# Eight weight tiles loaded ahead, two FFN tiles in the accumulators' PSUM banks, and a later start of batch 1's attention

## The chip, the cores and the metric

The kernel runs on one NeuronCore of a Trainium2 chip. The metric is device time in microseconds (us) of one execution; a kernel is told by the median of its runs. TensorE is called PE here, VectorE DVE, ScalarE ACT, GpSimd POOL and SyncE SP, as in the profile. Every bulk load and store is issued from SP's queue, in order.

## The reference

Inputs are q, k, v (8 batches, 8 heads, 576 positions, 64 per head), 32 packed queries p per head, and two FFN matrices w_in (512 x 2048) and w_out (2048 x 512). In short:

```
p_packed = softmax(p @ k.T / 8) @ v                      # 32 rows per head
a        = softmax(q @ p_packed.T / 8) @ p_packed        # 576 rows per head
x        = heads of a side by side                       # 4608 x 512
out      = softplus(x @ w_in) @ w_out                    # float32
```

The data are float64 in memory (the weights are read as int64 words); the result is float32.

## The kernel before

**Weights.** w_in and w_out come as 16 tiles each of 128 x 512 float64 values, 512 KB a tile, and are turned to float32 on the core by `convert` (L173): ACT reads the two halves of each word (`first`: L200 writes m, L204 writes r), DVE builds sign and exponent (L206, L211), POOL adds (L219) into `w_in_sb` or a scratch tile t; for w_out, ACT rounds t to `wo_h` (L238) and DVE takes the remainder `wo_l` (L244). Tiles are numbered n = 0 to 31 in the order i0 i1 o0 o1 i2 i3 o2 o3 i4 i5 and so on. `prefetch` loads a tile into one of the places of the list `places` (L180): two buffers "x" and two stretches of the tile `rest`, which batch 0's softplus fills only later. When `first(n)` has read a place, the place is loaded again as long as n is below its entry in `until`.

**Attention.** For each batch, attention runs in a generator (`attention_first` for batches 0 and 1): it transposes the heads of k (`psT_k` on PE, copied to `T_k` by ACT, L268), takes scores against p, a softmax over 576 positions, packs v, then the same for q (`psT_q`, `T_q`) with a softmax over 32 columns on DVE. k and v of batch 0 lie in the four buffers of the pool `ld`, q of batch 0 in a part of `w_in_sb` not yet used; batch 1's k and v take the same four buffers. `weights` splits the result into `at_h` (ACT, L525) and `at_l` (DVE, L526).

**FFN.** For each batch there are 16 units f. `make_m` (L535) folds p_packed into w_in: `psm` on PE (L543), split into `mh` by ACT (L558) and `ml` by DVE (L559); for batch 0 one call serves two units. `gemm1` (L564) makes `ph` in two halves of 288 columns, 12 matmuls (L580). `softplus` (L597) is Abs (L602), Exp (L604) and Ln (L605) on ACT, then max-and-add on DVE (L607), which is the last reader of `ph`, then the split into `gh` and `gl` (L594, L595); POOL saves 64 columns (L611). Two units later (LAG) `gemm2_tile` (L616) adds gh, gl times wo_h, wo_l into four accumulators `acc`, 12 matmuls of 512 columns (L618).

**PSUM.** There are eight banks: four for `acc` (pool `ps_acc`), two for `ph` (pool `ps_h`, tag "h"), two for everything else (pool `ps_m`, tag "m": `psm`, `psT`, scores, `psa`, `psp`, `psx`). During attention 0 the six banks of `ps_acc` and `ps_m` are lent in turn (`bank`, L87); `spare.clear()` (L712) ends that.

**Order of the work.** PE's order is the order of the program text. In the main loop (L717) each unit has four t-steps; at each one gemm2 tile is issued, `due` grows by PACE (0.56; in batch 1's units by PACE_FIRST, 0.62) and, whenever it passes 1, one step of the next batch's attention is issued; in batch 0 `cdue` grows by 1.6 and issues steps of `convert`. The other engines' order is chosen by the framework's scheduler from that program; each engine then works its queue strictly in order.

Of the kernel before, what the change touches and what calls it, by code (L numbers as in the profile page):

```python
# [9 lines left out]
F32 = mybir.dt.float32  # L10
# [5 lines left out]
I64 = mybir.dt.int64  # L16
# [10 lines left out]
def pack_attention_then_softplus_ffn(  # L27
# [14 lines left out]
    P = 128  # L42
# [4 lines left out]
    G = H * J // P  # L47
    HG = H // G
    NF = DFF // P
    NT = S // P  # L50
    REST = S - NT * P
    LAG = 2
    MC = 512
    Q = 32
    FIRST = 2
# [3 lines left out]
    ld = ctx.enter_context(tc.tile_pool(name="ld", bufs=2 * G))  # L59
# [3 lines left out]
    ps_acc = ctx.enter_context(tc.tile_pool(name="ps_acc", bufs=NT, space=bass.MemoryType.PSUM))  # L63
    ps_h = ctx.enter_context(tc.tile_pool(name="ps_h", bufs=2, space=bass.MemoryType.PSUM))
# [82 lines left out]
    CN = 512  # L147

    def load64(srcs, nm, place):
        if place is None:  # L150
            x = cv.tile([P, CN], I64, tag="x", name=f"x_{nm}", bufs=2)
        else:
            x = rest[:, place:place + 8, :].rearrange("x f j -> x (f j)").bitcast(I64)
        n = P // len(srcs)
        for i, src in enumerate(srcs):
            nc.sync.dma_start(
                x[i * n:(i + 1) * n].rearrange("x (a n) -> x a n", a=src.shape[1]), src
            )
        return x
# [13 lines left out]
    def convert(order):  # L173
# [3 lines left out]

        srcs = {"i": w_in_src, "o": w_out_src}

        places, until = [None, None, LAG, LAG + 8], [len(order), len(order), 6, 16]  # L180
        xs, ts, rs, at = {}, {}, {}, {}

        def prefetch(place):
# [39 lines left out]
        for n in range(2):  # L223
            prefetch(n)
        yield
        for n in range(2, 4):
            prefetch(n)
        yield
        for n in range(len(order) + 1):
# [6 lines left out]
            t = ts.pop(n - 1)[0].bitcast(F32) if n else None  # L236
# [327 lines left out]
    def gemm1(b, f, res):  # L564

        n = m_cols(b)
        halves = res["m"][f * P // n]
        at_h, at_l = res["at"]
        phs = []
        for c in range(2):  # L570
            ph = ps_h.tile([P, 512], F32, tag="h", name=f"ph_{b}_{f}_{c}")
            phs.append(ph[:, :C])
            i = 0
            for g in range(G):
                mh, ml = halves[g * n // MC]
                o = g * n % MC + f * P % n
                ms = slice(o, o + P)
                cs = slice(c * C, (c + 1) * C)
                for x, y in ((mh, at_h), (mh, at_l), (ml, at_h)):
                    nc.tensor.matmul(  # L580
                        ph[:, :C], x[:, ms], y[:, g, cs],
                        start=(i == 0), stop=(i == 3 * G - 1),
                    )
                    i += 1
        return phs
# [83 lines left out]
    order = []  # L669
# [4 lines left out]
    PACE = 0.56  # L674
    FRONT = 1000
    PACE_FIRST = 0.62
    CONV = 1.6
    CONV_EARLY = 1.6
    CONV_STEP = 14
# [15 lines left out]
    due = 0.0  # L695
# [18 lines left out]
    gs, acc = {}, None  # L714
    units = [(b, f) for b in range(B) for f in range(NF)]
    ahead, chain, due = iter(()), iter(()), 0.0
    for u in range(len(units) + LAG):  # L717
        if u < len(units):
            b, f = units[u]
            if f == 0:  # L720
                if (b + 1) % BG == 0 and b + 1 < B:
                    pack_transposed((b + 1) // BG, pt)
                ahead = attention(b + 1) if b + 1 < B else iter(())
                due = 0.0
            chain = softplus(b, f, gemm1(b, f, res[b]), gs)
            next(chain)
            if f == NF - 1:
                if (b + 2) % BG == 0 and b + 2 < B:
                    pt = load_pack((b + 2) // BG, (nc.sync,))
                for _ in ahead:  # L730
                    pass
                if b + 1 < B:
                    weights(b + 1)
        if u >= LAG:
            b2, f2 = units[u - LAG]
            gh, gl = gs.pop((b2, f2))
            if f2 == 0:
                acc = [ps_acc.tile([P, DM], F32, tag="acc", name=f"acc_{b2}_{t}") for t in range(NT)]
        last = u >= LAG and f2 == NF - 1 and b2 % 2 == 1
        if last:  # L740
            both = rests(b2)
            next(both)
        for t in range(NT):
            if u >= LAG:
                gemm2_tile(
                    acc[t], gh, gl, f2, slice(t * P, (t + 1) * P), f2 == 0, f2 == NF - 1
                )
                if f2 == NF - 1:
                    store(acc[t], [(0, b2, t * P, P)], f"{b2}_{t}", t)
            if u < len(units):  # L750
                due += PACE if b != FIRST - 1 else PACE_FIRST
                while due >= 1:
                    next(ahead, None)
                    due -= 1
                if b == 0:
                    cdue += CONV
                    while cdue >= 1:
                        next(conv, None)
                        cdue -= 1
            next(chain, None)  # L760
        if last:
            next(both)
        if u + 2 < len(units):


            nb, c = units[u + 2][0], units[u + 2][1] * P
            if c % m_cols(nb) == 0:
                make_m(nb, c // m_cols(nb), res[nb])
# [29 lines left out]
```

## Time and profile before

| | |
|---|---|
| runs | 777.18, 774.43, 775.15 us; median 775.15 |
| profiled execution | 774.48 us, its span 772.7 us (1.8 us lie around the span) |
| busy over the span | PE 94%, DVE 68%, ACT 56%, POOL 13% |
| mean granted PE clock | 0.985 |

Times in the views are us from the span's start. A row of the timeline has start, duration, engine, line, operation, output and input; a bracket tells the idle time ahead of it on its engine and who ended that. A row of the stages has, for each engine, the busy us and the number of instructions; PEclk is the granted clock, 1.00 being full speed. A row of the waits has total us, times, and the longest.

### The profile page before, as it was taken

The page shows a single profiled execution, that of the slowest core. Times are in us where ns is not written, and L with a number is a line of the kernel's source. Part 1 is how long each engine was busy: PE and PEld are TensorE (multiplying, and loading weights), DVE is VectorE, ACT ScalarE, POOL GpSimd, SP SyncE. Part 2 cuts the span into 40 slices and gives each one's busy share as a digit, 9 for nine tenths or more (in the row PEclk, how much of TensorE's full clock was granted, in tenths as well). Part 3 has the DMA queues.
Part 4 walks back from the last instruction along what each step waited for, and adds up shares of the span by engine and source line. Part 5 has one row for each costly group of instructions (what it writes and reads, how often), then busy time and mean ns, then how long its engine had stood idle before and what let it go on. Part 6 is the DMA issues. An engine that isn't in the chain of part 4 may idle for free.

```text
span 772.7 us, 14153 instructions
## 1 busy us (share of the span) xinstructions
PE 729.3 (94%) x5360; PEld 577.0 (75%) x5360; DVE 527.4 (68%) x1092; ACT 435.3 (56%) x1057; POOL 99.0 (13%) x166
## 2 busy tenths in 40 slices
PE   6457997999999999999999999999999999999997
PEld 4346675687788778877887777878787777888886
DVE  2697869975877559575877559576877558565554
ACT  5667977666455445565555455565555355555540
POOL 1253434200000000000010000000010000000110
PEclk9969999999999999999999999999999999999999
DMA  9977644534302342052402332043401400010002
GB/s 205 247 194 179 180 133 125 120 74 78 76 17 68 63 68 57 1 116 47 87 0 69 62 63 62 1 98 51 92 1 55 75 2 1 1 55 1 1 1 68
DMA packets 149668, 55.97 MB, mean 72 GB/s; under 512 B 116320, under 2 KB 142944, under 8 KB 149600
## 3 DMA queue, kind: packets, MB, share of 16 engines
q1 hardware_dynamic: 149328, 55.00, 31.9%
q8 instruction: 42, 0.69, 0.4%
q14 instruction: 26, 0.21, 0.1%
q10 hardware_dynamic: 272, 0.07, 0.0%
HBM read 45.61 MB, written 9.44 MB: 71 GB/s over the span
## 4 chain that ended last, share of the span: by engine, by line
PE 82%; DVE 6%; ACT 6%; DMA 4%; POOL 1%; issue 1%; SPq 0%; ACTq 0%; DVEq 0%; POOLq 0%
PE acc L618 41%; PE ph L580 26%; PE acc_m L618 6%; PE psm L543 4%; PE ps L275 2%; DMA w_in_sb<-in_q 2%; PE psp L318 1%; PE psa L308 1%; DMA k<-in_k 1%; ACT m L200 1%; DVE at_l L526 1%; DVE t L211 1%; POOL t L219 1%; ACT e L604 1%; DVE t L206 1%
## 5 line engine op out<-in xcount | busy, mean ns | idle before, releaser
L602 ACT ACTIVATE e<-ph 128x288 f32<-128x288 f32 x256 | 103.1, 404 | 189.3 <-PE ph L580 142.4
L618 PE MATMUL acc<-wo_h,gh 128*128 128x512 f32 x512 | 207.6, 405 | 0.0
L607 DVE SCALAR_TENSOR_TENSOR e<-ph,e 128x288 f32<-128x288 f32 x256 | 113.3, 451 | 131.9 <-ACT e L605 128.2
L618 PE MATMUL acc<-wo_l,gh 128*128 128x512 f32 x512 | 200.9, 392 | 0.0
L618 PE MATMUL acc<-wo_h,gl 128*128 128x512 f32 x512 | 200.8, 392 | 0.0
L580 PE MATMUL ph<-at_h,mh 128*128 128x288 f32 x512 | 158.9, 310 | 14.8 <-ACT at_h L525 7.5
L580 PE MATMUL ph<-at_l,mh 128*128 128x288 f32 x512 | 153.3, 299 | 3.7 <-DVE at_l L526 3.7
L580 PE MATMUL ph<-at_h,ml 128*128 128x288 f32 x512 | 152.7, 298 | 0.0
L580 PEld LDWEIGHTS ph<-at_h,mh 128*128 128x128 f32 x512 | 97.6, 191 | 48.8 <-DVE e L607 10.8
L611 POOL COPY rest<-e 128x64 f32<-128x64 f32 x128 | 53.2, 416 | 575.8 <-DVE e L607 544.2
L618 PEld LDWEIGHTS acc<-wo_h,gh 128*128 128x128 f32 x512 | 96.2, 188 | 27.4 <-issue 10.2
L618 PEld LDWEIGHTS acc<-wo_h,gl 128*128 128x128 f32 x512 | 96.1, 188 | 21.0
L604 ACT ACTIVATE e<-e 128x288 f32<-128x288 f32 (+1 forms) x240 | 109.5, 456 | 3.9
L605 ACT ACTIVATE e<-e 128x288 f32<-128x288 f32 (+1 forms) x240 | 109.4, 456 | 3.2
L618 PEld LDWEIGHTS acc<-wo_l,gh 128*128 128x128 f32 x512 | 96.4, 188 | 13.0
L580 PEld LDWEIGHTS ph<-at_l,mh 128*128 128x128 f32 x512 | 97.8, 191 | 8.2 <-DVE at_l L526 5.3
L580 PEld LDWEIGHTS ph<-at_h,ml 128*128 128x128 f32 x512 | 97.8, 191 | 0.0
L595 DVE TENSOR_TENSOR gl<-e,gh 128x512 fp32r<-128x512 f32 x128 | 87.7, 685 | 5.5
L558 ACT CAST mh<-psm 128x512 fp32r<-128x512 f32 (+1 forms) x72 | 35.9, 540 | 53.5 <-PE psm L543 53.4
L594 DVE CAST gh<-e 128x512 fp32r<-128x512 f32 x128 | 55.5, 434 | 5.1
L559 DVE TENSOR_TENSOR ml<-psm,mh 128x512 fp32r<-128x512 f32 (+1 forms) x72 | 42.8, 623 | 20.2 <-ACT mh L558 19.6
L543 PE MATMUL psm<-w_in_sb,pt 64*32 64x512 f32 (+1 forms) x576 | 40.0, 560 | 9.7 <-ACT T_k L268 4.8
(79 smaller groups left out, 693.5 us busy)
## 6 DMA issues: line engine op xcount, KB each, us to landing
v<-in_v SPq DMA_DIRECT2D x16, 576.0 KB, 5.0
x_i<-in_moe_w_in SPq DMA_DIRECT2D x28, 256.0 KB, 4.5
k<-in_k SPq DMA_DIRECT2D x48, 144.0 KB, 3.1
q<-in_q SPq DMA_DIRECT2D x48, 144.0 KB, 3.2
x_o<-in_moe_w_out SPq DMA_DIRECT2D x11, 512.0 KB, 3.8
out<-o SPq DMA_DIRECT2D x18, 256.0 KB, 2.5
rest<-in_moe_w_out SPq DMA_DIRECT2D x5, 512.0 KB, 6.0
k<-in_k SPq DMA_DIRECT2D x4, 576.0 KB, 6.5
```

The lines of the kernel that those rows point to most:

```text
L543: nc.tensor.matmul(ps[hh * J:(hh + 1) * J, :n], res["pt"][g][o:o + D, hh * J:(hh + 1) * J], w_in_sb[o:o + D, hh, c * n:(c + 1) * n], start ...
L558: nc.scalar.copy(mh[:, cols], ps[:, :n])
L559: nc.vector.tensor_tensor(ml[:, cols], ps[:, :n], mh[:, cols].bitcast(F32), op=ALU.subtract)
L580: nc.tensor.matmul(ph[:, :C], x[:, ms], y[:, g, cs], start=(i == 0), stop=(i == 3 * G - 1),)
L594: nc.vector.tensor_copy(hi, x)
L595: nc.vector.tensor_tensor(lo, x, hi.bitcast(F32), op=ALU.subtract)
L602: nc.scalar.activation(es[c], hv[c], AF.Abs)
L604: nc.scalar.activation(x, x, AF.Exp, scale=-1.0)
L605: nc.scalar.activation(x, x, AF.Ln, bias=1.0)
L607: nc.vector.scalar_tensor_tensor(es[c], hv[c], 0.0, es[c], op0=ALU.max, op1=ALU.add)
L611: nc.gpsimd.tensor_copy(rest[:, rest_at(b, f), r:r + REST], e[:, NT * P:])
L618: nc.tensor.matmul(acc, x[:, cs], y[:, f, :], start=(first and i == 0), stop=(last and i == 2),)
```

## The change

Three things are changed.

1. **Places for weight tiles.** The list gets four more entries, "ld", which are the four buffers of k and v of batch 0 (a tile of the pool `ld`, tag "ld"). At the start n = 0, 1 go to "x", n = 2, 3 to `rest`, and n = 4 to 7 (i2, i3, o2, o3) each to a buffer of k or v as soon as batch 0's attention has read that for the last time. These four are used once (`until` 0). The first stretch of `rest` is not loaded again (`until` 2 instead of 6). The places "x" then hold n = 8 and 9 where they held 4 and 5.
2. **Banks.** `ph` of units 0 and 1 of batch 0 is taken from `ps_acc` instead of `ps_h`.
3. **Pace.** In batch 0's units, which issue batch 1's attention, `due` does not grow in the first 8 t-steps (AFTER), so that attention starts with unit 2 instead of unit 0; from there it grows by PACE_FIRST (0.62) per t-step instead of PACE (0.56). Batch 1's units keep 0.62 and the later ones 0.56.

What it moves on PE: batch 1's first transposes of k stand in unit 2 instead of behind unit 0, its second scores of the first half (`scores2`, g = 0) at the end of unit 10 instead of unit 9, those of the second half in unit 13 instead of 12. The six later `psm` pairs of batch 0 (pairs 2 to 7) each stand directly behind another user of the two "m" banks; before, three of the seven pairs from 1 on did so (1, 3 and 5). The rows below show PE and ACT at the places that matter; the names are the program's, with the batch's or unit's number behind them.

PE, from the end of unit 0's gemm1, before (`k` is batch 1's; `psm_1` feeds units 2 and 3):

```order
72 L580 MATMUL ph_0_1_534<-at_h_521,ml_0_0_516 128x288
73 L262 MATMUL psT_k_0_0_551<-ident,k_0_497 128x96 x3
74 L262 MATMUL psT_k_0_1_573<-ident,k_0_497 128x96 x3
75 L543 MATMUL psm_1_0_587<-w_in_sb,pt_0_351 32x256 x4
76 L543 MATMUL psm_1_1_588<-w_in_sb,pt_1_428 32x256 x4
77 L580 MATMUL ph_1_0_603<-at_h_521,mh_0_0_515 128x288
```

and PE from the same place in the changed kernel:

```order
72 L584 MATMUL ph_0_1_536<-at_h_523,ml_0_0_518 128x288
73 L546 MATMUL psm_1_0_575<-w_in_sb,pt_0_354 32x256 x4
74 L546 MATMUL psm_1_1_576<-w_in_sb,pt_1_430 32x256 x4
75 L584 MATMUL ph_1_0_591<-at_h_523,mh_0_0_517 128x288
76 L584 MATMUL ph_1_0_591<-at_l_524,mh_0_0_517 128x288
```

The two transposes have gone from between gemm1 of unit 0 and `psm_1`; units 1 and 2 now follow without any work of attention.

ACT, from the Ln of unit 0 on, before (m and r read weight tiles, `mh_1` is the split of `psm_1`):

```order
62 L605 ACTIVATE e_0_541<-e_0_541 128x576
63 L268 COPY T_k_0_0_555<-psT_k_0_0_551 128x288
64 L200 ACTIVATE m_557<-x_i_288 128x512
65 L204 ACTIVATE r_559<-x_i_288 128x512
66 L268 COPY T_k_0_1_577<-psT_k_0_1_573 128x288
67 L204 ACTIVATE r_581<-rest 128x512
68 L558 CAST mh_1_0_597<-psm_1_0_587 128x256
```

and ACT in the changed kernel:

```order
62 L609 ACTIVATE e_0_543<-e_0_543 128x576
63 L203 ACTIVATE m_551<-x_i_174 128x512
64 L207 ACTIVATE r_553<-x_i_174 128x512
65 L207 ACTIVATE r_569<-rest 128x512
66 L561 CAST mh_1_0_585<-psm_1_0_575 128x256
```

The two copies T_k have gone; the weight tiles' reads are the same and in the same order as before (the order of ACT, DVE and POOL is unchanged up to here).

ACT in unit 4 of the changed kernel, around the copies of the first scores (`ps_1_0_0` and `ps_1_0_1` hold both "m" banks; `psT_k_1_0`, `psT_k_1_1` and `psm_3` need them next):

```order
97 L287 COPY a_1_0_673<-ps_1_0_0_824 128x288
98 L207 ACTIVATE r_711<-x_o_620 128x512
99 L203 ACTIVATE m_709<-x_o_620 128x512
100 L608 ACTIVATE e_4_812<-e_4_812 128x576
101 L207 ACTIVATE r_771<-x_o_637 128x512
102 L609 ACTIVATE e_4_812<-e_4_812 128x576
103 L203 ACTIVATE m_769<-x_o_637 128x512
104 L241 CAST wo_h<-t_713 128x512
105 L287 COPY a_1_0_673<-ps_1_0_1_830 128x288
106 L271 COPY T_k_1_0_854<-psT_k_1_0_850 128x288
107 L271 COPY T_k_1_1_884<-psT_k_1_1_880 128x288
```

Seven instructions now stand between the two copies that set the banks free; on PE the pair `psm_3` stands directly behind `psT_k_1_1`.

```
-        if place is None:
+        if place == "x":
             x = cv.tile([P, CN], I64, tag="x", name=f"x_{nm}", bufs=2)
+        elif place == "ld":
+            x = ld.tile([P, CN], I64, tag="ld", name=f"x_{nm}")
...
-        places, until = [None, None, LAG, LAG + 8], [len(order), len(order), 6, 16]
+        places = ["x", "x", LAG, LAG + 8] + ["ld"] * 2 * G
+        until = [len(order), len(order), 2, 16] + [0] * 2 * G
...
-        for n in range(2, 4):
+        for n in range(2, len(places)):
...
-            ph = ps_h.tile([P, 512], F32, tag="h", name=f"ph_{b}_{f}_{c}")
+            pool, tag = (ps_acc, "acc") if b == 0 and f < LAG else (ps_h, "h")
+            ph = pool.tile([P, 512], F32, tag=tag, name=f"ph_{b}_{f}_{c}")
...
+    AFTER = 8
...
-                due += PACE if b != FIRST - 1 else PACE_FIRST
+                if b >= FIRST:
+                    due += PACE
+                elif b or NT * f + t >= AFTER:
+                    due += PACE_FIRST
```

## The prediction, made before the result was known

> **What bounds the kernel now.** I read the busy time by stages first, with a border where batch 1's first gemm1 starts (153.3 us).
>
> ```profile
> 43.80:61.00 17.20, 9.33 (x49) 7.26 (x50) 14.23 (x24) 11.60 (x24) 10.03 (x8) 0.70 0.85 210
> 61.00:75.40 14.40, 12.56 (x90) 9.58 (x89) 10.20 (x22) 11.69 (x26) 4.88 (x6) 0.90 0.63 164
> 75.40:126.00 50.60, 47.04 (x416) 35.46 (x417) 41.23 (x87) 41.20 (x87) 21.53 (x22) 1.00 0.57 152
> 126.00:153.30 27.30, 23.22 (x163) 16.98 (x161) 25.75 (x51) 19.12 (x38) 8.61 (x9) 1.00 0.56 125
> 43.80:153.30 109.50, 92.15 (x715) 69.28 (x715) 91.41 (x181) 83.61 (x173) 45.05 (x42) 0.94 0.62 156
> 153.30:772.70 619.40, 613.56 (x4396) 491.52 (x4396) 412.82 (x861) 325.06 (x828) 46.09 (x113) 1.00 0.23 47
> ```
>
> After 153.3 us PE is busy 613.56 of 619.4 us: that part is PE's own work, and the change touches none of it. Batch 0's FFN (43.8 to 153.3) is different: PE is idle 17.4 us of 109.5, at clock 0.94, while DVE is busy 91.41 and ACT 83.61, since weight conversion, softplus and batch 1's attention meet there. So the time moves only by as much as the 153.3 moves. Who holds PE in that stretch, by the waits of PE:
>
> ```profile
> PE ph L580 <- DVE e L607: 7.2, 4, 3.0
> PE psm L543 <- ACT T_k L268: 4.8, 2, 4.5
> PE psm L543 <- ACT T_q L268: 2.5, 2, 1.7
> PE psm L543 <- POOL w_in_sb L219: 1.7, 1, 1.7
> PE psm L543 <- ACT a1T L309: 0.7, 1, 0.7
> ```
>
> Two PSUM shortages are seen. `ph` has two banks, so a unit waits until the unit before has been read by L607 (7.2 us). `psm` shares the two "m" banks with attention and waits for ACT's copies T_k, T_q, a1T (8.0 us, and 1.7 for a weight tile; 9.7 in all). PE's timeline shows the places:
>
> ```profile
> 45.88 1.07 PE L262 MATMUL psT_k<-ident,k 96*128 96x96 f32 x6
> 51.49 1.07 PE L543 MATMUL psm<-w_in_sb,pt 64*32 64x256 f32 x8 [4.55 <-ACT T_k L268]
> 53.85 0.61 PE L580 MATMUL ph<-at_h,mh 128*128 128x288 f32 x1
> 60.64 0.61 PE L580 MATMUL ph<-at_h,mh 128*128 128x288 f32 x1 [3.05 <-DVE e L607]
> 63.45 0.44 PE L580 MATMUL ph<-at_h,ml 128*128 128x288 f32 x1
> 64.53 0.72 PE L275 MATMUL ps<-T_k,pT 64*32 64x288 f32 x16
> 66.66 0.41 PE L262 MATMUL psT_k<-ident,k 96*128 96x96 f32 x3
> 68.32 0.40 PE L580 MATMUL ph<-at_h,mh 128*128 128x288 f32 x1
> ```
>
> Unit 1 begins at 53.85, unit 2 at 60.64, unit 3 at 68.32.
>
> **Part 1, eight tiles in flight: 0.** It pays only where ACT waits for a weight tile. ACT's waits for loads from 28 to 160 us:
>
> ```profile
> ACT r L204 <- DMA x_o<-in_moe_w_out: 1.0, 1, 1.0
> ACT m L200 <- DMA x_i<-in_moe_w_in: 0.3, 1, 0.3
> ACT m L200 <- DMA rest<-in_moe_w_out: 0.2, 1, 0.2
> ```
>
> 1.5 us in all, and the longest is for a late load of w_out, whose place the change leaves as it was. The order rows show the same tiles read in the same order up to unit 1. So between 0 and 0.5 us can be gained; I take 0. It could also cost: the loads of i2 and i3 are now queued behind `rest` without waiting for ACT, and the critical chain of the first 22 us is the load of q:
>
> ```profile
> 6.90 14.82 DMA w_in_sb<-in_q
> ```
>
> The new loads stand behind q's on the same queue. If they took bandwidth from it, the part newly issued before 21.7 us (i3 and half of i2, about 0.8 MB) at the 210 GB/s of the first row would cost up to 3.7 us. I take 0, because i2 was on its way before q had landed in this run too; the upper end goes to the range. The Trainium skill (DMA: Bandwidth & Descriptors, "Two DMAs through the same engine are not ordered") says that descriptors of one queue start in order on each engine; by it q would lose nothing. No run here shows that yet.
>
> On SP's queue, behind the new waits for v's buffers (read last by `psp`), stand i4, i5, o4 and batch 1's k; all are needed only after 40 us, so no one waits.
>
> **Parts 2 and 3 in the front.** ACT, DVE and POOL around unit 0's softplus:
>
> ```profile
> 49.86 0.62 ACT L238 CAST wo_h<-t 128x512 fp32r<-128x512 f32 x1 [0.79 <-POOL t L219]
> 50.39 0.68 ACT L605 ACTIVATE e<-e 128x576 f32<-128x576 f32 x1
> 50.97 0.38 ACT L268 COPY T_k<-psT_k 128x288 f32<-128x288 f32 x1
> 51.25 0.68 ACT L200 ACTIVATE m<-x_i 128x512 f32<-128x512 f32 x1
> 51.83 0.68 ACT L204 ACTIVATE r<-x_i 128x512 int32<-128x512 uint32 x1
> 52.39 0.40 ACT L268 COPY T_k<-psT_k 128x288 f32<-128x288 f32 x1
> 51.10 0.82 DVE L607 SCALAR_TENSOR_TENSOR e<-ph,e 128x288 f32<-128x288 f32 x2
> 53.90 0.68 DVE L595 TENSOR_TENSOR gl<-e,gh 128x512 fp32r<-128x512 f32 x1
> 54.50 0.41 DVE L559 TENSOR_TENSOR ml<-psm,mh 128x256 fp32r<-128x256 f32 x1
> 65.80 0.82 DVE L607 SCALAR_TENSOR_TENSOR e<-ph,e 128x288 f32<-128x288 f32 x2 [2.04 <-ACT e L605]
> 44.48 1.32 POOL L219 TENSOR_TENSOR w_in_sb<-t,r 128x512 int32<-128x512 int32 x1 [3.63 <-DVE t L211]
> ```
>
> - Until 46.1 us (end of unit 0's gemm1) nothing changes: the orders are the same.
> - `psm_1` then runs at 46.1, where `psT_k` stood (45.88): its weights are there (POOL ends at 44.48 + 1.32 = 45.8). Two halves of 1.07 end at 48.2. Unit 1 has its own banks: 12 matmuls at (63.45 - 60.64) / 11 = 0.255 us give 51.3.
> - Unit 2 needs `ml_1`. ACT reaches `mh_1` two T_k copies (0.28 each from start to start) earlier, near 52.7; DVE still passes L607, conversion and gl first and makes the first `ml_1` at 54.5 and the second directly behind it, at 54.9. Unit 2's third matmul starts at 54.95; ten at 0.24 end it near 57.3. Before, it ended at 63.45 + 0.44 = 63.9.
> - Unit 3 needs unit 2's L607. Before, that ended at 66.62, 2.7 us behind unit 2's end. In the new order two instructions of conversion on ACT and one on DVE stand in between (0.58 + 0.53 + 0.6 = 1.7): 57.3 + 2.7 + 1.7 = 61.7. PE meanwhile does four gemm2 tiles and two transposes (57.3 to 60.7) and `psm_2`.
>
> Unit 3 starts at 61.8 instead of 68.3: 6.5 us earlier. But PE has by then done three transposes (0.25 each) and one set of scores (0.65) less of attention, 1.4 us, which comes later. **Front: -5.1 us.** The bounds: 0, if DVE and ACT hold the later units as late as before, and -6.5, if that 1.4 is hidden.
>
> The clock in the front, in stages of 2 us:
>
> ```profile
> 50.00:52.00 2.00, 0.51 (x8) 0.23 (x8) 1.88 (x5) 2.00 (x5) 1.48 (x1) 0.53 1.02 307
> 54.00:56.00 2.00, 2.00 (x9) 2.00 (x10) 1.93 (x4) 1.25 (x3) 1.60 (x1) 0.50 1.09 257
> ```
>
> After PE's pause (46.9 to 51.5) it works at about half clock, still so at 54 to 56. In the changed kernel a pause stays between units 1 and 2 (51.3 to 54.95), so I count units 1 and 2 at half clock, as measured. The Trainium skill (TensorE: Matmul & The Clock Gate, "What's actually happening") halves the clock after an idle window of about 3.4 us and restores it after a busy one of that length; the rows agree. By it the pause of 3.6 us could fall either way; at full clock unit 2 would end 1.2 us earlier and the sum would be -5.3 instead of -4.1.
>
> **Part 3 later on: the "m" banks.** Now six pairs of `psm` stand directly behind another user of the banks. What one such place costs:
>
> ```profile
> 108.56 0.64 PE L543 MATMUL psm<-w_in_sb,pt 64*32 64x256 f32 x8 [0.80 <-ACT T_q L268]
> 121.34 0.67 PE L543 MATMUL psm<-w_in_sb,pt 64*32 64x256 f32 x16 [1.71 <-ACT T_q L268]
> ```
>
> I take 0.2 for pair 2 (PE arrives late there), 0.8 for pairs 4, 5 and 7, 1.7 for pair 6 (both banks are held by scores that DVE must read), and for pair 3 this: between the two copies of the scores stand seven instructions of ACT (four m or r at 0.58, Exp and Ln at 0.58, wo_h at 0.53: 4.0 us), in which PE has three gemm2 tiles and a transpose, 2.3 us; 1.7 more of wait and 0.8 for the copies behind it, 2.5. Sum 6.8. The pairs 2 to 7 waited 9.7 - 4.8 = 4.9 before: **+1.9 us** (bounds: 0, and +5.4 if each of the six costs 1.7).
>
> **The end of batch 0.** From 126 to 153.3 DVE is busy 25.75 of 27.3 us and PE idle 4.1: the last weight tiles and the second softmax meet. In the new order that softmax begins behind the last weight tile's instruction on DVE, one unit later. 1.7 of the 4.1 is the wait for a weight tile, counted above; of the other 2.4 I take **-0.9** (bounds 0 and -2.4), as only one unit's overlap goes.
>
> Does the softmax then come too late for batch 1? Between the transposes of its scores and the second `at_l` DVE has 17 instructions of at most 0.68 and two tiny ones, under 12 us, and no conversion. PE has in that time two gemm2 tiles of unit 13, units 14 and 15, `psm` and `ppt`, with full units as here:
>
> ```profile
> 157.90 1.58 PE ph L580 x12
> 159.48 2.74 PE acc L618 x12
> ```
>
> 1.4 + 2 x 4.3 + 1.0 + 0.6 = 11.6. That is about even: 0, with up to +1.
>
> **Sum:** 0 - 5.1 + 1.9 - 0.9 = -4.1 us. The profiled execution took 774.48 (span 772.7); it would take 770.4. It lies 0.67 below the median, and I set the forecast from the median: 775.15 - 4.1 = 771.0 us. About 0.5%, 3.9 us, is what a measurement of this kernel can tell from no change, so faster means below 771.3: the forecast lies just beyond that line.
>
> **Rivals.**
> - *The lead is spent waiting (no change).* ACT and DVE have the same work in batch 0 as before, 83.61 and 91.41 us, and PE's lead only makes it wait for them in units 3 to 12. For: over 75.4 to 126 each of the two is busy 81%. Against: DVE was free 4.2 of the 14.4 us from 61 to 75.4, which the new order uses. It would give -1 to 0: 774.5.
> - *All of the front is kept and the end gains too.* Bank waits as before (4.9), the end -2.4: -5.1 - 2.4 = -7.5: 767.6. For: DVE's heavy part comes when conversion is over. Against: the pair `psm_3` in the order.
> - *The banks make it slower.* Each of the six pairs waits for ACT copies that stand behind conversion, as pair 1 did for 4.8 us. The point of no gain is a mean of (4.9 + 5.1) / 6 = 1.7 us per pair; at 3.1 the six make 18.6, so 18.6 - 4.9 - 5.1 = +8.6: 783.8; at 2.4, +4.4: 779.5, which I take as its time. For: 1.71 has been seen. Against: of the five places in the waits only one was over 1.7.
>
> **How the numbers follow.** Forecast 0.50 (its own range 768.8 to 773; 0.33 of it below 771.3), all kept 0.18, no change 0.22, slower 0.10. Faster 0.33 + 0.18 = 0.51; within 0.5% 0.17 + 0.22 = 0.39; slower 0.10. The range takes in the first three and the q term only in part: 766.2 to 775.8.
>
> **What would show it.** Right: `psm_1` within 0.5 us of unit 0's end, unit 1 directly behind it, unit 2 ending near 57 and unit 3 starting near 62; no wait for L607 before unit 1 or 2; a wait of some 2 us around `psT_k_1_1` and `psm_3`; batch 1's gemm1 starting near 149.2. Wrong: q landing later than 22 us (part 1 costs), unit 3 near 62 but batch 1 at 152 or later (the lead is spent), waits at `psm` of over 10 us (the banks), or batch 1's gemm1 waiting for `at_l`.

## The result, and the profile after

The changed kernel takes 779.16 us (median of 4 runs, 778.62 to 779.37), the kernel before 774.79 (4 runs): 1.0051 times as long (95% interval 1.0031 to 1.0071), 4.4 us slower, where I had forecast 4.1 us faster. Its profiled execution has a span of 776.8 us against 772.7.

By stages, as before, with the border where batch 1's first gemm1 starts (157.38 us now; a row has, for PE, PEld, DVE, ACT and POOL, busy us and instructions, then PE's granted clock, DMA share and GB/s):

```profile
44.60:157.40 112.80, 96.78 (x715) 73.49 (x715) 93.94 (x181) 83.97 (x173) 42.97 (x42) 0.89 0.58 147
157.40:776.80 619.40, 613.55 (x4396) 491.55 (x4396) 412.94 (x861) 325.15 (x828) 46.23 (x113) 1.00 0.23 47
```

Batch 1 begins 4.1 us later (157.38 - 153.28), and that is the whole difference of the spans: behind it PE is busy 613.55 us of 619.40, as before. All of it arises up to the end of batch 0's FFN. PE's idle time there has not grown (112.80 - 96.78 = 16.0 us, before 17.4), but PE is busy 4.6 us longer for the same number of instructions, at clock 0.89 instead of 0.94.

PE's timeline shows the front as forecast, and then the waits (in the bracket: idle before, and who ended it):

```profile
46.78 1.11 PE L546 MATMUL psm<-w_in_sb,pt 64*32 64x256 f32 x16
53.94 0.61 PE L584 MATMUL ph<-at_h,mh 128*128 128x288 f32 x1 [3.81 <-ACT mh L561]
63.23 0.40 PE L584 MATMUL ph<-at_h,mh 128*128 128x288 f32 x1
76.93 0.74 PE L265 MATMUL psT_k<-ident,k 96*128 96x96 f32 x3 [3.02 <-ACT a L287]
107.13 0.64 PE L546 MATMUL psm<-w_in_sb,pt 64*32 64x256 f32 x8 [0.71 <-ACT a1T L312]
109.84 0.68 PE L546 MATMUL psm<-w_in_sb,pt 64*32 64x256 f32 x8 [2.07 <-DVE pt L336]
126.31 0.91 PE L546 MATMUL psm<-w_in_sb,pt 64*32 64x256 f32 x16 [2.38 <-DVE a L346]
140.18 0.84 PE L546 MATMUL psm<-w_in_sb,pt 64*32 64x256 f32 x16 [0.87 <-ACT T_q L271]
```

`psm_1` follows unit 0 directly, unit 3 starts at 63.23 (before 68.32), unit 4 at 68.27 (75.37): 5.1 and then 7.1 us ahead. Behind it come `psT_k_1_1`, the two halves of `psm_5`, `psm_6` and `psm_7`, which wait 9.05 us in all for the "m" banks. The first of these is the pair of scores that the prediction named. ACT's timeline there:

```profile
71.42 0.40 ACT L287 COPY a<-ps 128x288 f32<-128x288 f32 x1 [0.29 <-PE ps L278]
71.72 0.67 ACT L207 ACTIVATE r<-x_o 128x512 int32<-128x512 uint32 x1
72.29 0.66 ACT L203 ACTIVATE m<-x_o 128x512 f32<-128x512 f32 x1
...
75.96 0.62 ACT L241 CAST wo_h<-t 128x512 fp32r<-128x512 f32 x1 [0.63 <-POOL t L222]
76.48 0.39 ACT L287 COPY a<-ps 128x288 f32<-128x288 f32 x1
```

Seven instructions stand between the two copies, which start 5.1 us apart; `psT_k_1_1` needs the second. The same in windows of 3.41 us (PE's busy us and instructions, the granted clock, DMA share, GB/s), round `psm_5`:

```profile
103.49:106.90 3.41, 2.78 (x14) 1.00 0.41 104
106.90:110.31 3.41, 1.10 (x16) 1.00 0.15 43
110.31:113.73 3.42, 3.42 (x17) 0.50 0.45 111
113.73:117.14 3.41, 3.41 (x61) 1.00 0.72 197
```

A window with much waiting is followed by one at half clock. That happens behind the waits at 76.9 (two windows), 109.8 and 126.3; in the profile of before it does not happen once behind 64 us.

From unit 3's start to batch 1, PE alone, before and then after:

```profile
68.32:153.28 84.96, 75.48 (x616) 1.00 0.59 149
```

```profile
63.23:157.38 94.15, 82.92 (x636) 0.93 0.54 140
```

The changed kernel enters this stage 5.1 us ahead and needs 9.2 us more for it: 1.75 more idle (11.23 against 9.48), 7.44 more busy. Of the latter some 1.4 is attention put off from the front; the rest, 6.0, is put down to half clock. The idle time grew by so little, in spite of the 9.05 us at the "m" banks, because other waits went: those for the product's last reader (L607, now L611) fell from 4.2 to 1.5 us here, and the wait of 1.7 us for a weight tile is gone.

### The profile page after: what moved, and what is told of

Same layout as the page of the kernel before. It is cut to its first block, busy times and chain, and to the rows that moved or that the text cites. A ratio compares the mean times of both kernels' runs of the same rounds, so it can differ in the third digit from the quotient of the medians.

```text
span 776.8 us, 14159 instructions
## 1 busy us (share of the span) xinstructions
PE 733.9 (94%) x5360; PEld 580.9 (75%) x5360; DVE 530.0 (68%) x1092; ACT 435.7 (56%) x1057; POOL 97.0 (12%) x166
## 4 chain that ended last, share of the span: by engine, by line
PE 82%; DVE 8%; ACT 4%; DMA 3%; issue 1%; POOL 1%; SPq 0%; ACTq 0%; DVEq 0%; POOLq 0%
PE acc L622 41%; PE ph L584 26%; PE acc_m L622 6%; PE psm L546 4%; PE ps L278 2%; DMA rest<-in_moe_w_out 2%; PE psp L321 1%; DVE at_l L529 1%; PE psa L311 1%; DVE t L214 1%; DMA x_i<-in_moe_w_in 1%; DVE e L611 1%; ACT e L608 1%; DVE t L209 1%; DVE gl L599 1%
## 5 line engine op out<-in xcount | busy, mean ns | idle before, releaser
L611 DVE SCALAR_TENSOR_TENSOR e<-ph,e 128x288 f32<-128x288 f32 x256 | 113.2, 451 | 132.9 <-ACT e L609 131.7
L599 DVE TENSOR_TENSOR gl<-e,gh 128x512 fp32r<-128x512 f32 x128 | 90.5, 707 | 5.6
L562 DVE TENSOR_TENSOR ml<-psm,mh 128x512 fp32r<-128x512 f32 (+1 forms) x72 | 42.6, 622 | 20.0 <-ACT mh L561 19.3
```

What stands on the lines that cost most here:

```text
L562: nc.vector.tensor_tensor(ml[:, cols], ps[:, :n], mh[:, cols].bitcast(F32), op=ALU.subtract)
L599: nc.vector.tensor_tensor(lo, x, hi.bitcast(F32), op=ALU.subtract)
L611: nc.vector.scalar_tensor_tensor(es[c], hv[c], 0.0, es[c], op0=ALU.max, op1=ALU.add)
```

## The experiments

The theory after the traces, **A**: the places directly ahead of `psm` make PE wait for the two "m" banks, the clock halves behind each wait, and that takes the front's gain back and more. The rivals: **B**, part 1 (the places of the weight tiles) costs time all through batch 0; **C**, ACT and DVE limit batch 0, so that a lead can only be spent. Each run is timed against the kernel before in the same session, and the ratio is to that.

### The three parts alone

e1_places has part 1 alone, e2_banks part 2, e3_pace part 3, e4_banks_pace parts 2 and 3. Their diffs against the kernel before are pieces of the change:

```diff
e1:
-        places, until = [None, None, LAG, LAG + 8], [len(order), len(order), 6, 16]
+        places = ["x", "x", LAG, LAG + 8] + ["ld"] * 2 * G
+        until = [len(order), len(order), 2, 16] + [0] * 2 * G
...
e2:
+            pool, tag = (ps_acc, "acc") if b == 0 and f < LAG else (ps_h, "h")
...
e3:
+    AFTER = 8
...
+                elif b or NT * f + t >= AFTER:
+                    due += PACE_FIRST
e4: the lines of e2 and e3
```

> The kernel before with the first part of the change alone: eight weight tiles in flight, the attention and the banks as before. Theory A (the m banks): the change loses behind its front, where psT_k_1_1, psm_3, psm_5 and psm_6 wait for the two m banks and the granted clock falls to half after each wait; this part adds only the 0.8 us by which gemm1 of unit 0 starts later (39.48 against 38.71): 775.6, between 774.8 and 776.6. Theory B (the places): the two weight tiles that land 0.7 to 0.9 us later push conversion back all through batch 0, and this part makes up most of the 4.4 us by which the changed kernel is slower: 777.5 or more. Theory C (the lead is only spent, since ACT and DVE limit batch 0): 774.8 to 775.6, as A.

> The kernel before with the second part alone: the gemm1 of units 0 and 1 in the accumulators' banks, the attention's places as before. psm_1 still waits 4.8 us behind psT_k_0_0 and psT_k_0_1, so that unit 1 starts no earlier; only unit 2 no longer waits for unit 0's product at L607, which stands behind psm_1's wait anyway. Theory A: -0.5 to -2 us, 773 to 774.3, since the order at the later m banks is that of before. Theory B: 774.8, no change. Theory C: 774.3 to 774.8.

> The kernel before with the third part alone: batch 1's attention begins two units later and goes at 0.62, places and banks as before. Theory A: psm_1 runs directly behind unit 0, but units 1 and 2 wait in the h banks for the products of the unit before, so that some 2 to 4 us of the front's 5.1 are won; the later m-bank waits and their half clock are those of the changed kernel (9 us lost from unit 4 on, as it was 7.1 ahead there and ends 4.1 behind less the 0.8 of its start): 778 to 781, slower. Theory B: below 776, since the places are not there. Theory C: 774 to 775.5.

> The changed kernel without its first part: six weight tiles' places as before, units 0 and 1 in the accumulators' banks, the attention later. Theory A: 0.8 us below the changed kernel, 778.0 to 778.8, with waits of 2 us or more at psT_k_1_1 or psm_3, at psm_5 and at psm_6, each with a stretch at about half clock. Theory B: 774 to 776, the loss gone with the places. Theory C: 774.8, no change.

| run | median us | ratio (95%) | unit 0 | unit 3 | batch 1 |
|---|---|---|---|---|---|
| before | 775.52 | 1 | 38.71 | 68.32 | 153.28 |
| e1_places | 778.44 | 1.0040 (1.0026 to 1.0054) | 38.21 | 69.06 | 156.20 |
| e2_banks | 782.94 | 1.0093 (1.0080 to 1.0107) | 39.12 | 64.59 | 160.97 |
| e3_pace | 782.49 | 1.0089 (1.0073 to 1.0105) | 38.63 | 65.27 | 160.44 |
| e4_banks_pace | 777.93 | 1.0035 (1.0021 to 1.0050) | 38.30 | 62.44 | 155.94 |

(Starts of gemm1 in the profiled executions.) B falls as the main cause: most of the loss is there without part 1 (e4). But e1 came out where B had put it, and above A's range: part 1 alone costs 2.9 us. In its profile they are lost late: unit 10 starts at 114.07 (before 114.61), unit 12 at 129.99 (128.82), and two windows at half clock lie there, from 123.05 and from 136.70. And what I took for part 1's cost, unit 0's late start in the changed kernel's profile (39.48), is chance: in the changed kernel, e1 and the runs e5 to e8 below, all with part 1, unit 0 starts at 38.15 to 39.48, mean 38.56; in the kernel before, e2 to e4, e9 and e10, without it, at 38.26 to 39.12, mean 38.60. Whether part 1 costs something later in the changed kernel stays open: e4 and the changed kernel differ by 1.2 us, but their intervals overlap.

The parts do not add up: 2.9 + 7.4 + 7.0 us, but 4.4 together. A met e4, missed e1 and e3 by less than 2 us, and e2 by 9 us: in e2 the attention stands where it stood before, unit 3 is 3.7 us ahead, and batch 1 is 7.7 us behind. Its first loss is not at an "m" bank ahead of `psm`:

```profile
77.88 0.72 PE L275 MATMUL ps<-T_k,pT 64*32 64x288 f32 x5 [3.29 <-ACT T_k L268]
```

So every one of these kernels with an earlier unit 3 lost that lead, and not all at the same place.

### Is it the half clock?

e8_fill adds matmuls to the changed kernel that nobody reads, in free columns of the h banks, so that PE is busy while it waits. Two stand ahead of `psT_k_1_1`, three behind `psx` and three behind the second scores. The instructions of ACT, DVE and POOL stay in the changed kernel's order.

```diff
+    def fill(b, n):
+        at_h, _ = res[b]["at"]
+        for i in range(n):
+            nc.tensor.matmul(
+                full[i % 2][:, C:], at_h[:, 0, :P].bitcast(F32),
+                at_h[:, 0, :512 - C].bitcast(F32), start=True, stop=True,
+            )
...
+                if b == 0 and t == NT - 1 and f == 4:
+                    fill(0, 2)
...
+                if b == 0 and t == NT - 1 and f in (8, 10):
+                    fill(0, 3)
```

> The changed kernel with eight more matmuls in batch 0, whose results nobody reads, in free columns of the h banks: two ahead of psT_k_1_1 in unit 4, three between psx and psm_5 in unit 8, three ahead of psm_6 in unit 10. They stand where TensorE waits (3.0, 2.8 and 2.4 us) and should take some 0.6 us each. The order on the other engines is that of the changed kernel. Theory A1 (the clock): in all six traces so far the granted clock is 0.5 for whole stretches of 3.41 us on a fixed grid, each behind a stretch of 3.41 us in which TensorE was busy for less than about 0.55 of the time. With the waits filled, the stretches at 76 (two), 110 and 127 us should stay at 1.00: 775 to 777, 2 to 4 us less than the changed kernel's 779.2. Theory A2 (only the waits cost, the clock does not matter since ACT and DVE are the limit behind them): 778.5 to 780. The matmuls of the waits run longer than the wait: 780 or more.

Measured: 778.97 us (1.0049, 1.0036 to 1.0061), no gain. The fill did what it should at `psm_5` (windows of e8_fill, as above):

```profile
108.39:111.81 3.42, 2.72 (x24) 1.00 0.28 87
111.81:115.22 3.41, 3.41 (x23) 1.00 0.40 83
```

The window with the wait is now busy for 2.72 us, and the next keeps its clock; unit 9 takes 5.8 us to unit 10 instead of 7.2. At `psT_k_1_1` it did so only in part: the fill itself stood 1.43 us until DVE had read the h bank that it writes, the window of the wait was busy for 1.57 us, and one half-clock window follows instead of two. At `psm_6` PE is let go at 126.92 (126.31 in the changed kernel), without a half-clock window behind it; and a new one turns up from 87.9, so that two are left of four. In the whole stage:

```profile
63.41:157.72 94.31, 84.15 (x652) 0.96 0.53 136
```

Less 3.82 us of fill (1.02 + 1.40 + 1.40), PE is busy 80.3 us, 2.6 less than in the changed kernel; it waits, the fill counted in, 14.0 us instead of 11.2, 2.8 more. A1 is not borne out, and A2 met the time: the half clock is real, but the 2.6 us of it that went came back as waits. That fits PE being let go at times that other engines set; with two half-clock windows left and a fill that waits for DVE itself, the run does not prove it.

### Is it the places ahead of psm?

e6_gap ("the run without adjacent steps" in what was expected of others) is the changed kernel with one condition more, e5_after4 moves the attention's start, e7_first puts the copies that free the banks ahead of conversion (five places in batch 1's attention, one shown):

```diff
e6   -                while due >= 1:
     +                while due >= 1 and not (b == 0 and t == NT - 1 and f % 2 == 0):
e5   -    AFTER = 8
     +    AFTER = 4
e7   +        with tc.high_priority(offset=FRONT) if b == 1 else ExitStack():
             nc.scalar.copy(dst, ps[:, :C])
```

> The changed kernel, but in batch 0 no step of the attention stands directly ahead of a psm: a step that falls due there runs one gemm2 tile later. The order on ACT and DVE changes with it. Theory A (the m banks): the waits at psT_k_1_1, psm_5, psm_6 and psm_7, 9.0 us in the changed kernel, fall to under 3, with one half-clock stretch at most behind unit 4: 771 to 775. Theory C (ACT and DVE limit batch 0, the lead is only spent): TensorE waits as long in other places (L611, mh, at_l): 777 to 780.

> The changed kernel with AFTER = 4: batch 1's attention begins one unit earlier (one unit later than in the kernel before), and no step of it but two transposes of k at units 2 to 4 stands directly ahead of a psm. Theory A: as in the run without adjacent steps, 771 to 776. Theory C: 777 to 780. If the attention's lateness itself is the cost: about half of the change's loss, 776 to 777.

> The changed kernel with the copies that free the m banks in batch 1's attention (ACT's copies of T, of the scores and of a1T, DVE's transposes of the second scores and its copy pt) put ahead of conversion by priority. Theory A: TensorE's waits at the m banks fall from 9.0 to some 4 us with one or two half-clock stretches less, but conversion is later: 775 to 777.5. Theory C: the same work is done in another order, 778 to 780.

Measured: e6_gap 774.26 us (0.9994, 0.9985 to 1.0004), e5_after4 775.75 (1.0014, 1.0005 to 1.0023), e7_first 778.21 (1.0043, 1.0030 to 1.0055), the kernel before 774.95. With no step directly ahead of a `psm` (e6) the change loses nothing: 4.9 us less (779.16 to 774.26), with the reservation that the edit shifts rows of ACT and DVE too. Priority for the copies does not do it, as C had it; conversion then comes late, and `psm_7` waits 3.23 us for its weights from POOL.

The stage from unit 3 to batch 1 in e6_gap:

```profile
62.40:152.81 90.41, 79.77 (x643) 0.96 0.58 145
```

It has 6.8 us at half clock, as many as e8_fill, but waits 10.6 us where that waits 14.0. Against the changed kernel's stage (94.15 us, busy 82.92) it is 3.7 us shorter: PE waits only 0.6 less and is busy 3.2 less, with two half-clock windows instead of four. Yet e6_gap gains nothing on the kernel before, though unit 3 starts 5.9 us ahead. Its largest waits behind 60 us:

```profile
PE psT_k L265 <- ACT a L287: 4.1, 1, 4.1
PE psT_q L265 <- DVE a L346: 1.6, 1, 1.6
PE ps L278 <- DVE ml L562: 1.5, 2, 1.3
```

All three wait for an "m" bank that another step or a `psm` still holds. `psm` is let through at once now, and the attention waits in its stead: `psT_k_1_1` for 4.1 us, with two half-clock windows. So A's time came, but not its signs (waits under 3 us there, one such window at most). Unit 5 is 2.5 us ahead, batch 1 0.5.

e5_after4 is a warning too. In its order a gemm2 tile stands between every step and the next `psm`, as in e6_gap, and still `psm` waits 7.5 us in all for the "m" banks; the first two of these waits:

```profile
75.95 0.64 PE L546 MATMUL psm<-w_in_sb,pt 64*32 64x256 f32 x8 [1.46 <-ACT T_k L271]
78.36 1.08 PE L546 MATMUL psm<-w_in_sb,pt 64*32 64x256 f32 x8 [1.77 <-ACT T_k L271]
```

With almost as much wait at `psm` as the changed kernel has at the banks, e5_after4 is 3.4 us faster than that. So the places are part of the loss at most; that they alone are its cause is not shown. For the lead C holds so far.

### Where does the lead go?

e9_gap6 is e6_gap without part 1; e10_gap_scores puts ACT's copies of batch 1's first scores first, which takes away the 4.1:

```diff
e9   the condition of e6 in e4_banks_pace
e10  +        with tc.high_priority(offset=FRONT) if b == 1 else ExitStack():
                 nc.scalar.copy(a1[:, c * C:(c + 1) * C], ps)
```

> The run without adjacent steps, with six weight tiles in flight as before (no part 1); the order on ACT and DVE is nearly that of that run (774.26). If part 1 costs the same here as in the changed kernel (779.16 with it, 777.93 without): 773.0, faster than the kernel before by some 0.25%. If the places cost nothing when the banks don't bind: 774.3. If the late tiles hid something, and conversion is starved without them: 775 or more.

> As the run without adjacent steps and with six tiles, and ACT's copies of batch 1's first scores go ahead of conversion. In the run without adjacent steps psT_k_1_1 still waits 4.12 us for the second copy, which stands behind four m and r and one wo_h that waits for POOL, and two half-clock stretches follow. If that wait is what spends the front's lead of 6 us: 2 to 4 us less, 769.5 to 771. If the lead is spent by ACT and DVE whatever waits first (theory C): the wait turns up again at later units, 772.5 to 774.5.

Measured: 774.84 us (0.9987, 0.9972 to 1.0002) and 774.93 (0.9987, 0.9973 to 1.0000), the kernel before 775.62. With part 1 (e6_gap, 0.9994) and without it (e9_gap6) the ratios cannot be told apart. In e10 unit 5 starts at 77.14, 5.8 us ahead of before (82.9); by unit 8 the lead is 1.6, and batch 1 starts at 155.27 in its profile, 2.0 behind. The wait taken away came back in pieces, as C said.

Which engine? e11_gap_light and e12_before_light spare DVE:

```diff
-                    wo_l[:, i, :], t, wo_h[:, i, :].bitcast(F32), op=ALU.subtract
+                    wo_l[:, i, :16], t[:, :16], wo_h[:, i, :16].bitcast(F32), op=ALU.subtract
+    nc.gpsimd.memset(wo_l.bitcast(F32).rearrange("x f e -> x (f e)"), 0.0)
```

> The run without adjacent steps, but wo_l is computed for 16 of its 512 columns only and is zero elsewhere (the low halves of the second weights are left out): 16 instructions of DVE of 0.6 us become some 0.1, about 8 us less of DVE in batch 0. Theory C, with DVE as the limit: the front's lead is kept in part, 2 to 5 us below 774.3: 769 to 772. If ACT's queue is what spends the lead: 773.5 to 775.

> The control: the kernel before with wo_l for 16 of its 512 columns only, zero elsewhere. Theory C: DVE limits the kernel before in batch 0 too, which shows as 1 to 3 us less: 772 to 774. If DVE's work is hidden there: 774.5 to 775.5. A larger gain here than in the run without adjacent steps would say that the front's lead is not spent on DVE.

Measured: 776.41 us (1.0007, 0.9994 to 1.0020) and 778.12 (1.0019, 1.0002 to 1.0037). Both are flawed by my own edit: the zeroing takes POOL 6.93 us and stands ahead of the identity matrix, so that unit 0 starts 1.6 and 2.6 us later. From unit 0 to batch 1 they take 115.7 and 116.2 us, against 114.5 (e6_gap) and 114.6 (before), though DVE is busy 7.8 and 6.7 us less in them. Sparing this work of DVE brought nothing; with the flaw, and one profile of each, that is a hint and no proof that DVE is not the limit.

e13_gap_nopool leaves out POOL's add, e14_gap_nor also ACT's `r`, both in e9_gap6; e15_before_nor and e16_after_nor are the kernel before and the changed kernel with both left out.

```diff
e13 to e16, in second(n):
+            if n >= 8:
...
+                nc.vector.scalar_tensor_tensor(
+                    o if a > 1 else o.rearrange("x (a n) -> x a n", a=a), x, 3, y,
+                    op0=ALU.logical_shift_left, op1=ALU.bitwise_or,
+                )
+                return
...
e14 to e16, in first(n):
+            if n < 8:
...
+                nc.scalar.activation(r, lo, AF.Copy, scale=2.0**-29)
```

> The run without adjacent steps and with six tiles (774.84, stage from unit 0's gemm1 to batch 1's 113.6 us in its profile), but POOL's add of the lowest three bits is left out for weight tiles 8 to 47, whose t comes from DVE's second instruction; ACT still makes r. If ACT's waits for POOL at wo_h (some 6 us behind 58 us) spend the lead: the stage is 3 to 6 us shorter, 769 to 772. If ACT's own work does: 774 to 775.5.

> As the run before, and ACT's r is left out too for tiles 8 to 47 (the weights are cut off instead of rounded in their last bits): 40 instructions of 0.58 us less on ACT, 23 us. If ACT's work spends the lead: 4 to 8 us below the run that only leaves out POOL's add, 766 to 770. If neither does, since each unit waits for a chain through all engines: within 1 us of it.

> The kernel before with r and POOL's add left out for tiles 8 to 47. If ACT and POOL are the limit of batch 0 before as well: 768 to 772. If PE's own waits at psm_1 and unit 2 are what costs before, and the rest is hidden: 773.5 to 775. The difference to the run without adjacent steps and without r is the worth of the front's lead when the limit is gone: 4 to 6 us by the prediction's front.

> The changed kernel with r and POOL's add left out for tiles 8 to 47. If conversion on ACT is what makes the m banks late in the changed kernel: 768 to 772, as good as the run without adjacent steps and without r plus at most 2 us. If the adjacent places cost their 3 to 5 us whatever ACT does: 4 us above that run.

There are 32 tiles, so the edit meets tiles 8 to 31: 24 instructions `r` at 0.58 us, some 14 us of ACT, and not 40 instructions and 23 us as the expectations have it.

| run | median us | ratio (95%) |
|---|---|---|
| e13_gap_nopool | 768.60 | 0.9910 (0.9893 to 0.9928) |
| e14_gap_nor | 767.27 | 0.9885 (0.9870 to 0.9900) |
| e15_before_nor | 764.09 | 0.9855 (0.9843 to 0.9868) |
| e16_after_nor | 768.97 | 0.9911 (0.9897 to 0.9925) |

By the ratios, POOL's add is worth 6 us in e9_gap6 (0.9987 to 0.9910); with `r` it is 8 there and 11 in the kernel before and in the changed one. So this chain limits batch 0. Two things go with the add, and these runs do not part them. ACT no longer stands at `wo_h` for it (6.4 us behind 58 us in e9_gap6). And DVE gets faster: in the stage from unit 3 to batch 1 it is busy 74.56 us for 153 instructions in e9_gap6, 69.86 us for 154 in e13. An add of POOL and the row of DVE that runs into it, from the changed kernel:

```profile
117.88 1.30 POOL L222 TENSOR_TENSOR w_in_sb<-t,r 128x512 int32<-128x512 int32 x1 [1.01 <-DVE t L214]
118.05 1.68 DVE L599 TENSOR_TENSOR gl<-e,gh 128x512 fp32r<-128x512 f32 x1
```

This `gl` takes 1.68 us; the same instruction takes 0.68 to 0.69 where POOL is at rest.

But the chain is not what the change loses: without it the changed kernel is still 4.9 us behind (768.97 against 764.09). My expectation for e15 (768 at least) was off by 4 us, and the front's lead does not show here either: e14 is 3.2 us behind e15.

With conversion light the stage from unit 3 to batch 1 reads well (e15_before_nor, then e16_after_nor, with the largest waits of PE behind 60 us):

```profile
66.27:142.98 76.71, 74.89 (x615) 1.00 0.65 165
```

```profile
PE ph L591 <- DVE e L618: 0.7, 2, 0.5
PE psm L554 <- ACT T_q L279: 0.5, 1, 0.5
```

```profile
62.56:148.92 86.36, 80.01 (x637) 0.96 0.60 152
```

```profile
PE psm L557 <- DVE a L357: 1.9, 1, 1.9
PE psm L557 <- ACT a1T L323: 1.2, 1, 1.2
PE psm L557 <- DVE pt L347: 0.9, 1, 0.9
PE psa L322 <- ACT a L298: 0.8, 1, 0.8
```

In the order of before PE waits 1.8 us in all, in the new order 6.35, and most of it at `psm` or a step of the attention; two half-clock windows follow at 117. e14_gap_nor, without steps ahead of `psm`, still idles 6.25 us (83.54 us, of which PE is busy 77.29), mostly at steps of the attention that wait for an "m" bank. Its largest:

```profile
PE psT_q L273 <- DVE ml L570: 1.9, 1, 1.9
PE ph L592 <- DVE e L619: 1.0, 1, 1.0
PE psT_q L273 <- DVE a L354: 1.0, 1, 1.0
```

The same number of steps in fewer units uses the two banks more densely. That led to the last two: e17_spread_nor (e14_gap_nor) and e18_spread (e9_gap6) begin the attention in unit 1 and go slower, so that its steps stand apart.

```diff
-    PACE_FIRST = 0.62
-    AFTER = 8
+    PACE_FIRST = 0.58
+    AFTER = 4
```

> The run without adjacent steps, r and POOL's add (767.27; TensorE idle 6.2 us from unit 3 to batch 1), with batch 1's attention from unit 1 on at 0.58 instead of from unit 2 at 0.62, so that hardly two steps of it stand together. If the squeezed attention spends the lead: the idle time falls to 2 or 3 us and the front's lead is kept, 762 to 764.5, at or below the kernel before without r (764.09). If the front itself loses by the earlier start, or other waits take the place: 766 to 768.

> The same order with all of conversion (the run without adjacent steps with six tiles, 774.84, with batch 1's attention from unit 1 on at 0.58). If the squeezed attention spends the lead here too: 771 to 773, faster than the kernel before. If conversion's chain through ACT and POOL is the limit whatever the attention does: 774 to 775.5.

Measured: e17 764.47 us (0.9856, 0.9834 to 0.9877), e18 779.24 (1.0051, 1.0033 to 1.0069), the kernel before 775.0. With light conversion, spreading gives 2.8 us (767.27 to 764.47; the intervals of the two just overlap), the time that was expected if the squeezed attention spends the lead, and PE's idle time falls to 3.75 us (2 or 3 expected):

```profile
64.07:143.12 79.05, 75.30 (x635) 1.00 0.65 161
```

The lead is not kept even so: unit 3 starts 2.2 us ahead of e15_before_nor (64.07 against 66.27), batch 1 at 143.12 against 142.98, with the clock at 1.00 in both. By the medians the 4.9 us between e16 and e15 split into some 1.7 for the places ahead of `psm` (768.97 to 767.27; part 1 is out too), 2.8 for the attention squeezed into fewer units, and 0.4; each step's intervals overlap, so the sizes are rough. With all of conversion the same order is 4.2 us slower than the kernel before, beyond both expectations. Its largest single wait behind 60 us is this one, PE's row and then ACT's:

```profile
122.93 0.67 PE L275 MATMUL ps<-T_q,pt 64*32 64x288 f32 x6 [3.40 <-ACT T_q L268]
```

```profile
119.27 0.62 ACT L238 CAST wo_h<-t 128x512 fp32r<-128x512 f32 x1 [2.36 <-POOL t L219]
...
122.49 0.38 ACT L268 COPY T_q<-psT_q 128x288 f32<-128x288 f32 x1
```

ACT stands 2.36 us at `wo_h` for POOL, and the last T_q copy is queued behind it. ACT's waits for POOL at `wo_h` from 58 to 153 us sum to 9.7 us here, to 11.2 in the changed kernel, and to 6.1 in the kernel before. Which order meets which of these waits is not settled by these runs; that stays open. e18_spread also has no step directly ahead of a `psm`, and is as slow as the changed kernel.

No version with all of the work is measurably faster than the kernel before: e9_gap6 and e10_gap_scores are at 0.9987 with intervals that reach 1.

## Why the prediction was wrong

- **Part 1, 0:** right at the start: PE first uses q at 20.14 to 21.72 us in the profiles with part 1 and at 20.17 to 21.86 in those without, so the loads behind q cost it nothing here, and unit 0 starts alike. Later it is open: part 1 alone costs 2.9 us (e1), and on top of the other two up to 1.2 that could not be told from nothing.
- **Front, -5.1:** unit 3 starts 5.1 us earlier (6.5 forecast; 0.8 of the difference is this execution's late unit 0), and every run with parts 2 and 3 has it. The events were right: `psm_1` behind unit 0, a pause ahead of unit 2 (3.81 us for mh and 0.98 for ml; 3.65 forecast), no wait for L611 ahead of units 1 and 2.
- **"m" banks, +1.9:** mis-sized. Pair 3 was forecast at 2.5 and took 3.02, pair 5 took 2.78 (0.8 forecast), pair 6 2.38 (1.7), pair 7 0.87 (0.8), pairs 2 and 4 nothing: 9.05 against 6.8. That alone would have left a gain: 4.15 more than before instead of 1.9. (The 4.9 of before that the sum takes off has 1.7 for a weight tile in it, which is no bank's.)
- **The step that failed is the sum.** It carried the front's -5.1 to the end as if only the rows named could touch it, and without a reason it left the clock out behind the front, as if at 1.00. In the profile that clock is the largest missing term: 6.0 us of half clock behind the waits, against 1.75 us more idle time. But the terms do not add: in the fill run 2.6 us of half clock went and the waits grew by 2.8.
- **What the runs show in its place.** The lead is spent on the way. The prediction's sign for that came: unit 3 at 63.23, batch 1 at 157.38. The run without adjacent steps has a lead of 5.9 us at unit 3 and 0.5 at batch 1, though no `psm` waits (774.26), and with light conversion e17_spread_nor spends its 2.2 us at full clock. The first rival, "the lead is spent waiting", names this; its price, 774.5, does not hold the loss of 4.4 us. Conversion's chain through ACT, POOL and DVE limits batch 0 (e13 to e16), and with light conversion so does, by rough sizes, how densely the attention uses the "m" banks. Why the changed order with all of conversion ends 4.4 us behind, and not level, stays open: the steps ahead of `psm` are part of it at most.
- **Rival "the banks make it slower"** (0.10, 779.5): the time came out at 779.16, but by luck. The pairs waited 9.05 / 6 = 1.5 us each, below its break-even of 1.7 and far from the 2.4 that its time needs.
- **End of batch 0, -0.9:** from unit 11's start to batch 1 30.2 us (127.15 to 157.38), before 31.3 (121.94 to 153.28): 1.1 less, about right in size. PE's idle time there fell further, from 4.1 to 1.4 us, mostly the waits for L607 and for the weight tile, and half clock took part of that back. No wait for the second `at_l` is seen.

## What to carry to other kernels

Where four engines pass buffers round, a lead at the front is not a term of a sum: follow it unit by unit to the next place where another engine sets the release, and ask there who is queued ahead of the instruction that frees the buffer. A user of a shared bank one matmul tile ahead of the next user, instead of directly ahead, went with 4.9 us here (e6_gap), but one tile was not always enough (e5_after4, e18_spread); and squeezing a serial chain into fewer slots to clear the front cost time with light conversion, while spreading it cost time with all of it. So time such an order before you believe in it. And when a kernel is balanced like this, test each part alone: three parts that cost 3, 7 and 7 us made 4.4 together.

## What the runs showed of the hardware

The granted clock changes on a fixed grid of 3.41 us whose phase differs from one execution to the next. In 18 of the profiles (all but e11 and e12), from 58 to 160 us, there are 478 stretches of the grid at full clock: PE was busy for less than half in 25 of them, and 24 of these were followed by a stretch at 0.50; of 22 at 0.50 to 0.65, 8 were; of 431 above 0.65, none. From half clock it comes back after a stretch that was busy for 0.95 or more (33 of 34). So a wait of some 2 us is enough if it falls into one stretch, and the same wait can do nothing where the grid lies otherwise. The wait of 2.38 us at `psm_6` was the same in the changed kernel and in e4_banks_pace; here are their grids round it, the changed kernel first:

```profile
123.97:127.38 3.41, 1.07 (x17) 1.00 0.40 117
127.38:130.79 3.41, 3.41 (x14) 0.50 0.39 117
```

```profile
123.66:127.07 3.41, 1.94 (x24) 1.00 0.60 154
127.07:130.48 3.41, 3.41 (x21) 1.00 0.54 173
```

In e4 the wait lay across a border and the busy share of the longer part's stretch was 0.57. The Trainium skill (TensorE: Matmul & The Clock Gate, "What's actually happening") gives a free-running window of 3413 ns, and the grid agrees; it speaks of an idle window, while here a window that was busy for a third of its time was enough.

While POOL works, some instructions of DVE take longer. In the changed kernel, from 58 to 153 us, `gl` (L599) takes 0.685 us on the mean where no instruction of POOL runs beside it (6 of them) and 1.025 where one does (8), `t` (L209) 0.418 (11) and 0.655 (10); `ml` (L562) takes 0.41 to 0.42 either way.
